# Seven block products for eight in two of the four out-projection chunks of batches 2 to 7

## The chip, the cores and the metric

One Trainium2 chip, one of its cores. The kernel is one launch on that core. The metric is the device time of a run in microseconds; the profile is one further execution of the same program, with its own time.

## The reference

Eight batches of attention with a pack of 32 learned queries per head, and then a feed-forward layer with the activation h cos h:

```
scale = 1/sqrt(64)
sm_attn(q, k, v) = softmax(scale * q k^T) v
p_packed = sm_attn(p, k, v)             # p: 8 x 8 x 32 x 64;  k, v: 8 x 8 x 576 x 64
attn     = sm_attn(q, p_packed, p_packed)
x        = attn as 4608 x 512           # tokens x (heads * 64)
h        = x @ w_in                     # w_in 512 x 2048
out      = (h * cos(h)) @ w_out         # w_out 2048 x 512, output float32
```

## The kernel before, in words

Work goes batch by batch (576 tokens, eight heads). Everything is emitted in an order written out by hand: each engine takes its instructions in the order of the program, and tile pools add the waits. Matmul operands are bf16, sums fp32.

Per batch s:

- `load` (L84) brings k, q and v from HBM through GpSimd's DMA queue; `permute_v` (L77) reorders v on GpSimd into `vp`; `xbar` (L93) and `a1_xbar` (L156) transpose q, k and the first attention weights by DMA from SP's queue.
- `s1` (L129, L140): scores of the packed queries and their exponentials on ScalarE. `recips` (L151, L152): the inverse row sums r1 on VectorE, and rs1 = r1 * scale, also on VectorE. `pp` (L183): the packed values, copied to `ppT`.
- `ppw` (L207): packed values times w_in, in four blocks n of 512 columns, evacuated to `PPW` by L75 (ScalarE) or L77 (VectorE). So x @ w_in is never formed; the hidden product uses PPW.
- `s2` (L129, L225): scores of the queries, exponentials `a2u`. `sums2` (L233, L235): their sums per head by a matmul with a block of ones, and the logarithm in `lns` (SBUF, fp32). `normalise` (L241, L243): exp(-lns) on ScalarE, then a2n = a2u * r1 * that on VectorE, for the halves y = 0 and 1.
- `h_mm` (L256, L260, L263), 16 times, fc = 0 to 15: four matmuls of 288 columns to a `psA` tile, cos by ScalarE (a sine with a bias) and the product g = h cos h by VectorE to `gT` [128, 16, 576]. After fc 7 and 15 GpSimd copies the last 64 tokens to `joint` (L267), which holds the remainders of two batches.
- The out-projection, `out_gen` (L309): chunks of 128 tokens, each 16 matmuls of 512 columns over the 2048 hidden features, into an `ot` bank; then a copy to `osb` by ScalarE or VectorE and stores on SP's queue (L316). Odd batches have a fifth chunk, the joint one. The last joint chunk is done at the end in two column halves (`tail_chunk`, L295).

PSUM holds three `psA` tiles of two banks (pool A) and two `ot` banks (pool O). The out-projection of batch s-1 fills in between the steps of batch s: `fill(n)` emits its next n matmuls. Slot s is the loop at L523 and the function `slot` (L423): in the first part come s2, the last PPW blocks, s1 of batch s+1, sums2 and normalise, with fills between them; then 16 hidden products with fills after each, in proportion to a quota, and with hooks: at fc 5 `pp(s+1)`, at fc 10 two PPW blocks of batch s+1. `keep` fills are left for the start of the next slot, where `set_filler` finishes them and begins the next batch's.

```
        normalise(s)
        ACT.preload_act_table_set(SIN_SET)
        fill(13)
...
        slot(s, [(5, lambda: pp(s + 1, engs=(ACT, ACT))), (10, lambda: pw2(s + 1))] if nxt else [], 5, {10: 3})
```

Before batch 3 the slots are written out one by one, with more loads and transposes.

Of the kernel before, what the change touches and what calls it, by code (L numbers as in the profile page):

```python
# [15 lines left out]
def kernel(  # L16
# [10 lines left out]
    nc = tc.nc  # L27
    B, H, S, D = q.shape
# [5 lines left out]
    TP = S // C  # L34
    HS = S // 2
    PSUM = bass.MemoryType.PSUM
    EXP_SET = "natural_log_exp_and_others"
    SIN_SET = "trig_and_small"

    const = ctx.enter_context(tc.tile_pool(name="const", bufs=1))  # L40
    bf_pool = ctx.enter_context(tc.tile_pool(name="bf", bufs=1))
    vp_pool = ctx.enter_context(tc.tile_pool(name="vp", bufs=2))
    att_pool = ctx.enter_context(tc.tile_pool(name="att", bufs=1))
    a2n_pool = ctx.enter_context(tc.tile_pool(name="a2n", bufs=2))
    ppw_pool = ctx.enter_context(tc.tile_pool(name="ppw", bufs=2))
    g_pool = ctx.enter_context(tc.tile_pool(name="g", bufs=2))
    j_pool = ctx.enter_context(tc.tile_pool(name="joint", bufs=2))
    cos_pool = ctx.enter_context(tc.tile_pool(name="cos", bufs=3))
    o_pool = ctx.enter_context(tc.tile_pool(name="o", bufs=4))
# [8 lines left out]
    w_out_bf = const.tile([128, NFC, DM], BF16, name="w_out_bf")  # L58
    ident = const.tile([128, 128], BF16, name="ident")
# [3 lines left out]
    p_raw = const.tile([128, 2 * B, D], FP32, name="p_raw")  # L63
# [84 lines left out]
    def recips(b):  # L148
        r1[b] = small.tile([128, 2], FP32, name="r1")
        rs1[b] = small.tile([128, 2], FP32, name="rs1")  # L150
        V.reciprocal(r1[b], sums1[b])  # L151
        V.tensor_scalar(out=rs1[b], in0=r1[b], scalar1=scale, scalar2=None, op0=ALU.mult)  # L152
# [42 lines left out]
    def ppw(b, n, eng=None, own=False, later=False, cuts=((0, 512),)):  # L195
        if b not in PPW:
            PPW[b] = ppw_pool.tile([128, 2, DF], BF16, name="PPW", tag="PPW")
# [12 lines left out]
        def evacuate(cuts=cuts):  # L210
            if own or two:
                for a, z in cuts:
                    for y in range(2):
                        copy(eng[y] if two else eng, PPW[b][:, y, n * 512 + a:n * 512 + z], ps[y][:, a:z])
            else:
                copy(eng or (V, ACT)[n % 2], PPW[b][:, :, n * 512:(n + 1) * 512], t)
# [4 lines left out]
    def s2(b):  # L221
        a2u[b] = att_pool.tile([128, 2, S], BF16, name="a2u", tag="a2u")
        ps = scores(ppT[b % 2], xT["q", b])
        for y in range(2):
            ACT.activation(out=a2u[b][:, y].rearrange("p (e x) -> p e x", e=2),  # L225
                           in_=ps[y][:, :, 0:HS], func=AF.Exp, scale=rs1[b][:, y:y + 1])

    def sums2(b, y):
        if b not in lns:
            lns[b] = att_pool.tile([128, 2, S], FP32, name="lns", tag="lns")  # L230
        ps = psa()
        for e in range(2):
            nc.tensor.matmul(ps[:, e, 0:HS], ones_blk, a2u[b][:, y, e * HS:(e + 1) * HS],  # L233
                             start=True, stop=True)
        ACT.activation(out=lns[b][:, y].rearrange("p (e x) -> p e x", e=2),  # L235
                       in_=ps[:, :, 0:HS], func=AF.Ln)

    def normalise(b):
        a2n[b] = a2n_pool.tile([128, 2, S], BF16, name="a2n", tag="a2n")
        for y in range(2):  # L240
            ACT.activation(out=lns[b][:, y], in_=lns[b][:, y], func=AF.Exp, scale=-1.0)  # L241
        for y in range(2):
            V.scalar_tensor_tensor(out=a2n[b][:, y], in0=a2u[b][:, y], scalar=r1[b][:, y:y + 1],  # L243
                                   in1=lns[b][:, y], op0=ALU.mult, op1=ALU.mult)
# [3 lines left out]
    def h_mm(b, fc):  # L248
        if fc == 0:
            gT[b] = g_pool.tile([128, NFC, S], BF16, name="gT", tag="gT")  # L250
# [3 lines left out]
        for y in range(2):  # L254
            for e in range(2):
                nc.tensor.matmul(ps[:, e, 0:HS], PPW[b][:, y, fc * 128:(fc + 1) * 128],  # L256
                                 a2n[b][:, y, e * HS:(e + 1) * HS], start=(y == 0), stop=(y == 1))
        cs = cos_pool.tile([128, S], BF16, name="cosT")
# [12 lines left out]
    n_out, out_eng = [0], [V, ACT]  # L271

    def pieces_of(b, c):
        ob = out[b * S:(b + 1) * S, :].rearrange("(p c) d -> c p d", c=C)
        if c == 4:
            o0 = out[(b - 1) * S:b * S, :].rearrange("(p c) d -> c p d", c=C)
# [9 lines left out]
    def n_chunks(b):  # L286
        return 5 if b % 2 and b < B - 1 else 4

    def tail_chunk(b, c):
        osb = o_pool.tile([128, DM], FP32, name="osb")  # L290
        for i in range(2):
            cols = slice(i * 256, i * 256 + 256)
            ps = O.tile([128, 256], FP32, name="ot", tag="ot")
            for fc in range(NFC):
                nc.tensor.matmul(ps, joint[b // 2][:, fc, :], w_out_bf[:, fc, cols],  # L295
                                 start=(fc == 0), stop=(fc == NFC - 1))
            copy((ACT, V)[i], osb[:, cols], ps)
            for (a, z, rows), q in zip(pieces_of(b, c), (nc.sync, nc.scalar)):
                q.dma_start(out=rows[:, cols], in_=osb[a:z, cols])

    def out_gen(b):
        groups = [(0, 1), (2,), (3,)] if b == 0 else [(c,) for c in range(n_chunks(b))]
        for grp in groups:
            pss = {c: O.tile([128, DM], FP32, name="ot", tag="ot") for c in grp}
            for f0 in range(0, NFC, 4):
                for c in grp:
                    for fc in range(f0, f0 + 4):
                        w = joint[b // 2][:, fc, :] if c == 4 else gT[b][:, fc, c * 128:(c + 1) * 128]
                        nc.tensor.matmul(pss[c], w, w_out_bf[:, fc, :],  # L309
                                         start=(fc == 0), stop=(fc == NFC - 1))  # L310
                        if fc == NFC - 1:
                            osb = o_pool.tile([128, DM], FP32, name="osb")
                            copy(out_eng[n_out[0] % len(out_eng)], osb, pss[c])
                            n_out[0] += 1
                            for a, z, rows in pieces_of(b, c):
                                nc.sync.dma_start(out=rows, in_=osb[a:z, :])  # L316
                        yield
# [3 lines left out]
    def set_filler(b):  # L321
        fill(1000)
        filler[0] = out_gen(b)
        filler[1] = 16 * n_chunks(b)

    def fill(n):
        while n > 0 and filler[1] > 0:
            next(filler[0])
            filler[1] -= 1
            n -= 1  # L330

# [243 lines left out]
```

The softmax here doesn't subtract the row's maximum and nothing guards it: scores larger than these inputs give would overflow.

## Time and profile before

| | |
|---|---|
| time, median of 2 runs | 248.99 us (248.95 to 249.03) |
| profiled execution, its own time | 248.62 us |
| its span, first to last instruction | 246.8 us |
| granted TensorE clock | 1.00 |
| busy: TensorE, VectorE, ScalarE, GpSimd | 233.2, 165.2, 169.0, 57.7 us |
| out-projection matmul, 128x512 | 379 ns each, first input to last output |
| hidden matmul, 128x288 | 286 ns each |
| g = h cos h on VectorE, 128x576 | 755 ns each |
| cos on ScalarE, 128x576 | 652 ns each |
| osb copy 128x512: VectorE, ScalarE | 690, 581 ns |
| osb copy 128x256: VectorE, ScalarE | 424, 372 ns |
| PPW cast 128x1024 on VectorE | 1222 ns |
| permute_v on GpSimd, 96x3072 | 2751 ns |
| joint copy on GpSimd, 128x512 | 616 ns |

PE is TensorE's matmuls, PEld its weight loads, DVE is VectorE, ACT ScalarE, POOL GpSimd, SP the engine that issues most DMAs. Matmuls overlap, so the time of one is longer than the distance between two. A row of the timeline gives start, duration, engine, line, operation, the tiles written and read, and how many of them in sequence; in brackets, the idle time before it and who ended it.

### The profile page before, as it was taken

What the parts mean: (1) busy time and instruction counts of PE and PEld (TensorE: products, weight loads), DVE (VectorE), ACT (ScalarE), POOL (GpSimd) and SP (SyncE); (2) the same over time, 40 slices, a digit from 0 to 9 for tenths busy, and PEclk for the clock granted to TensorE, in tenths of its full rate; (3) what the DMA queues carried; (4) which work ended last, traced back from release to release, by engine and by line L of the source; (5) the groups of instructions that cost most, each with busy time, mean ns of one, the idle gap of its engine ahead of it and who ended that gap; (6) DMA issues with size and microseconds to landing.
All of it is one profiled execution on the core that took longest, in us unless ns stands there. A gap on an engine that the chain in (4) does not pass through costs nothing.

```text
span 246.8 us, 5023 instructions
## 1 busy us (share of the span) xinstructions
PE 233.2 (94%) x1996; PEld 130.9 (53%) x2029; DVE 165.2 (67%) x248; ACT 169.0 (68%) x282; POOL 57.7 (23%) x70
## 2 busy tenths in 40 slices
PE   8788799999999999999999999999999999999993
PEld 3454374566545654565446554565456554665452
DVE  3549987677658776678767766678766684886110
ACT  2369799877576787888787776888778684873000
POOL 8342533240400355004503105030500100001000
PEclk9999999999999999999999999999999999999999
DMA  6999999999899999999999997999571113111133
GB/s 90 202 203 206 205 206 228 194 241 151 179 202 184 192 175 214 218 198 142 222 211 187 172 201 91 198 166 171 109 154 27 45 43 84 43 31 57 47 84 85
DMA packets 64231, 37.36 MB, mean 151 GB/s; under 512 B 36848, under 2 KB 59632, under 8 KB 64208
## 3 DMA queue, kind: packets, MB, share of 16 engines
q0 software_dynamic: 23152, 18.75, 50.0%
q1 hardware_dynamic: 40624, 18.09, 35.1%
q8 instruction: 16, 0.26, 0.4%
q10 hardware_dynamic: 432, 0.20, 0.4%
q14 instruction: 7, 0.06, 0.1%
HBM read 37.22 MB, written 9.44 MB: 189 GB/s over the span
## 4 chain that ended last, share of the span: by engine, by line
PE 78%; DMA 12%; issue 2%; DVE 2%; ACT 2%; POOL 2%; DVEq 0%; POOLq 0%
PE ot L309 46%; PE psA L256 21%; DMA vbf<-in_v_dram 10%; PE psA L207 3%; DMA a1T<-a 2%; PE psA L129 2%; PE psA L183 2%; DVE gT L263 2%; PE ot L295 1%; PE psA L233 1%; ACT cosT L260 1%; POOL vp L77 1%; ACT ppT L75 1%; POOL kbf L84 1%; PE ot L104 0%
## 5 line engine op out<-in xcount | busy, mean ns | idle before, releaser
L309 PE MATMUL ot<-w_out_bf,gT 128*128 128x512 bf16 x482 | 127.5, 379 | 2.0 <-issue 1.1
L263 DVE TENSOR_TENSOR gT<-psA,cosT 128x576 bf16<-128x576 f32 x128 | 93.8, 755 | 28.9 <-ACT cosT L260 28.2
L260 ACT ACTIVATE cosT<-psA 128x576 bf16<-128x576 f32 x128 | 82.4, 652 | 24.6 <-PE psA L256 22.1
L256 PE MATMUL psA<-a2n,PPW 128*128 128x288 bf16 x512 | 83.8, 286 | 1.6 <-DVE gT L263 0.4
L309 PEld LDWEIGHTS <-gT 128*128 128x128 bf16 x512 | 47.8, 98 | 43.4 <-issue 6.7
L256 PEld LDWEIGHTS <-PPW 128*128 128x128 bf16 x512 | 49.3, 98 | 34.6 <-issue 3.9
L77 DVE CAST PPW<-psA 128x1024 bf16<-128x1024 f32 (+1 forms) x23 | 26.9, 1175 | 11.6 <-PE psA L207 11.5
L267 POOL COPY joint<-gT 128x512 bf16<-128x512 bf16 x16 | 9.9, 616 | 82.5 <-DVE gT L263 82.5
L77 DVE COPY osb<-ot 128x512 f32<-128x512 f32 (+1 forms) x22 | 14.9, 678 | 17.5 <-PE ot L309 7.7
L77 POOL COPY vp<-vbf 96x3072 bf16<-96x3072 bf16 x7 | 19.3, 2751 | 6.3 <-DMA vbf<-in_v_dram 6.3
L75 ACT COPY osb<-ot 128x512 f32<-128x512 f32 (+1 forms) x15 | 8.5, 567 | 15.3 <-PE ot L309 10.6
L243 DVE SCALAR_TENSOR_TENSOR a2n<-a2u,r,lns 128x576 bf16<-128x576 bf16 x16 | 12.3, 812 | 7.3 <-ACT lns L241 7.3
L235 ACT ACTIVATE lns<-psA 128x576 f32<-128x576 f32 x16 | 10.1, 650 | 7.1 <-PE psA L233 6.5
L140 ACT ACTIVATE a<-psA 128x576 bf16<-128x576 f32 x16 | 10.3, 647 | 6.7 <-PE psA L129 6.7
L309 PE MATMUL ot<-w_out_bf,joint 128*128 128x512 bf16 x47 | 12.8, 379 | 0.1
L225 ACT ACTIVATE a2u<-psA,rs 128x576 bf16<-128x576 f32 x16 | 11.0, 737 | 1.4 <-PE psA L129 1.3
L75 ACT CAST ppT<-psA 64x128 bf16<-64x128 f32 x24 | 6.2, 260 | 7.0 <-DVE ppT L77 5.9
L207 PE MATMUL psA<-w_in_bf,ppT 64*32 64x512 bf16 x224 | 10.1, 380 | 0.0
L241 ACT ACTIVATE lns<-lns 128x576 f32<-128x576 f32 x16 | 10.0, 676 | 0.0
L347 PE MATMUL ot<-wz 128*128 128x512 bf16 x23 | 7.7, 468 | 1.4 <-DVE wz L358 1.2
L527 POOL COPY gate<-kT 1x1 bf16<-1x1 bf16 x3 | 0.5, 181 | 32.3 <-DMA kT<-kbf 32.3
L183 PEld LDWEIGHTS <-vp 96*128 96x128 bf16 x192 | 6.5, 98 | 2.3 <-issue 1.2
(73 smaller groups left out, 152.7 us busy)
## 6 DMA issues: line engine op xcount, KB each, us to landing
kbf<-in_k_dram POOLq DMA_DIRECT2D x8, 576.0 KB, 12.6
vbf<-in_v_dram POOLq DMA_DIRECT2D x8, 576.0 KB, 7.6
qbf<-in_q_dram POOLq DMA_DIRECT2D x8, 576.0 KB, 10.1
out_dram<-osb SPq DMA_DIRECT2D x24, 192.0 KB, 2.7
out_dram<-osb SPq DMA_DIRECT2D x22, 128.0 KB, 2.4
w_in_bf<-in_moe_w_in_dram POOLq DMA_DIRECT2D x4, 512.0 KB, 17.3
w_out_bf<-in_moe_w_out_dram POOLq DMA_DIRECT2D x4, 512.0 KB, 21.2
out_dram<-osb SPq DMA_DIRECT2D x26, 64.0 KB, 2.1
```

The costliest lines, as they stand in the source:

```text
L75: ACT.copy(out=out, in_=in_)
L77: eng.tensor_copy(out=out, in_=in_)
L140: ACT.activation(out=a1[b % 2][:, y, :, 0:TP].rearrange("p (e m) x -> p e m x", e=2), in_=ps[y][:, :, 0:HS].rearrange("p e (m x) -> p e m ...
L183: nc.tensor.matmul(ps[:, hp * 64:(hp + 1) * 64], vp[b][:, c, hp * 128:(hp + 1) * 128], a1T[b][0:TP, :, j, 32 * hp:32 * hp + 32], start=(j ...
L207: nc.tensor.matmul(ps[y][32 * x:32 * x + 32, :], ppT[b % 2][r, 2 * x + y, :], w_in_bf[r, x, n * 512:(n + 1) * 512], start=True, stop=True)
L225: ACT.activation(out=a2u[b][:, y].rearrange("p (e x) -> p e x", e=2), in_=ps[y][:, :, 0:HS], func=AF.Exp, scale=rs1[b][:, y:y + 1])
L235: ACT.activation(out=lns[b][:, y].rearrange("p (e x) -> p e x", e=2), in_=ps[:, :, 0:HS], func=AF.Ln)
L243: V.scalar_tensor_tensor(out=a2n[b][:, y], in0=a2u[b][:, y], scalar=r1[b][:, y:y + 1], in1=lns[b][:, y], op0=ALU.mult, op1=ALU.mult)
L256: nc.tensor.matmul(ps[:, e, 0:HS], PPW[b][:, y, fc * 128:(fc + 1) * 128], a2n[b][:, y, e * HS:(e + 1) * HS], start=(y == 0), stop=(y == 1))
L260: ACT.activation(out=csv, in_=ps[:, :, 0:HS], func=AF.Sin, bias=PI_HALF)
L263: V.tensor_tensor(out=gT[b][:, fc, :].rearrange("p (e x) -> p e x", e=2), in0=ps[:, :, 0:HS], in1=csv, op=ALU.mult)
L309: nc.tensor.matmul(pss[c], w, w_out_bf[:, fc, :], start=(fc == 0), stop=(fc == NFC - 1))
```

## The change

**Block products.** For batches 2 to 7 (`FIRST = 2`), chunks 0 and 1 (256 tokens) are computed together. With the hidden features split in even and odd fc and the output columns in two halves of 256, the product is one of 2x2 blocks, and seven block products with sums before and after take the place of eight. A block product is 8 matmuls of 256 columns. Chunks 2 and 3 stay as they were; batches 0 and 1 stay as they were.

- Sums of w_out's blocks (T0 to T3, 2048 elements per partition each) are made once, on GpSimd, in slots 1 and 2; T3 takes over the buffer of `p_raw`.
- Sums of g's blocks (S1 to S4) are made per batch on GpSimd by `S_sums`, in two parts of 512 elements per partition each, so eight instructions, in `close`, right before the next batch's fills are set and before `permute_v`. For the last batch, parts of them come at fc 7 and 11 of slot 7.
- `pair_gen` emits the products in the order 1, (2, 6), 7, (4, 5), 3, each group in one `ot` bank. Product 1 is copied to `m1`; the others are combined by VectorE sums that read PSUM and an SBUF operand (`plus`).

**Order of the out-projection.** A batch's fills are now: one column half of a joint chunk (batches 1 to 6), the direct chunks, then the pair. `fill` counts half passes: 2 for a 512-column matmul, 1 for a 256-column one. `keep` is 10 halves (5 passes before). In a slot the fills are emitted before the product g where there is no hook.

**Other edits.** rs1 = r1 * scale is made by ScalarE (`scaled`), at hook 2 of the slot before. From batch 3 on the logarithms and inverse sums stay in PSUM, in place of `lns`. The two halves of a2n are emitted after 4 and 8 of 13 fills, not together. PPW is four tiles of 512 columns rather than two of 2048; `vp` has one buffer rather than two. From batch 2 on the copy of a chunk is on VectorE in the first part of a slot and on ScalarE in the hidden products, as before, and at the end on ScalarE alone.

The core of the diff:

```diff
-    vp_pool = ctx.enter_context(tc.tile_pool(name="vp", bufs=2))
+    vp_pool = ctx.enter_context(tc.tile_pool(name="vp", bufs=1))
-    ppw_pool = ctx.enter_context(tc.tile_pool(name="ppw", bufs=2))
+    ppw_pool = ctx.enter_context(tc.tile_pool(name="ppw", bufs=4))
...
+    def scaled(b):
         rs1[b] = small.tile([128, 2], FP32, name="rs1")
-        V.reciprocal(r1[b], sums1[b])
-        V.tensor_scalar(out=rs1[b], in0=r1[b], scalar1=scale, scalar2=None, op0=ALU.mult)
+        ACT.activation(out=rs1[b], in_=r1[b], func=AF.Copy, scale=scale)
...
+        else:
+            lns[b, y] = ps[:, :, 0:HS]
...
+    def S_sums(b, p, eng, k0, k1, which=(0, 1, 2, 3)):
...
+        t = S[b, p]
+        A11, A12 = (A_blk(b, 2 * p, i, k0, k1) for i in range(2))
+        A21, A22 = (A_blk(b, 2 * p + 1, i, k0, k1) for i in range(2))
+        S1, S2, S3, S4 = (t[:, i, k0:k1, :] for i in range(4))
+        for i in which:
+            out, in0, in1, op = ((S1, A21, A22, ALU.add), (S2, S1, A11, ALU.subtract),
+                                 (S3, A11, A21, ALU.subtract), (S4, A12, S2, ALU.subtract))[i]
+            eng.tensor_tensor(out=out, in0=in0, in1=in1, op=op)
...
+    def pair_gen(b, p):
...
+        m = {1: (A11, B_blk(0, 0)), 2: (A12, B_blk(1, 0)), 3: (S4, B_blk(1, 1)),
+             4: (A_blk(b, 2 * p + 1, 1, 0, 8), T[3]), 5: (S1, T[0]), 6: (S2, T[1]), 7: (S3, T[2])}
+
+        def then_double(ps):
+            plus(o2, ps, u3)
+            store(o2, 2 * p + 1)
+            plus(o1[:, 2], ps[:, 1], o1[:, 2])
+
+        def then_last(ps):
+            plus(o1[:, 1], ps, o1[:, 2])
+            store(o1, 2 * p)
+
+        then = {1: lambda ps: copy(out_eng[0], m1, ps), 2: lambda ps: plus(o1[:, 0:3:2, :], ps, m1),
+                7: lambda ps: plus(u3, ps, o1[:, 2]), 4: then_double, 3: then_last}
+
+        for names in ((1,), (2, 6), (7,), (4, 5), (3,)):
+            ps = O.tile([128, 2, 256], FP32, name="ot", tag="ot")
+            for i, n in enumerate(names):
+                lhs, rhs = m[n]
+                for kp in range(8):
+                    nc.tensor.matmul(ps[:, i], lhs[:, kp, :], rhs[:, kp, :], start=kp == 0, stop=kp == 7)
+                    if kp == 7 and n == names[-1]:
+                        then[names[0]](ps if i else ps[:, 0])
+                    yield 1
...
+    def out_gen(b):
+        for j, i in joints_of(b):
+            yield from joint_half(j, i, store_half(j))
+        if b < FIRST:
+            yield from direct_gen(b, ((0, 1), (2,), (3,)) if b == 0 else ((0,), (1,), (2,), (3,)))
+        else:
+            yield from direct_gen(b, ((2,), (3,)))
+            yield from pair_gen(b, 0)
...
-            h_mm(s, fc)()
+            rest = h_mm(s, fc)
...
+            if not (hooks and hooks[0][0] == fc):
+                fill_halves(quota)
+                rest()
...
+    def close(s):
+        fill(1000)
+        if s >= FIRST:
+            for g in ((6, 8),) if s == B - 1 else ((0, 4), (4, 8)):
+                S_sums(s, 0, G, *g)
+        set_filler(s)
...
-        fill(1000)
-        set_filler(s - 1)
+        close(s - 1)
         if nxt:
             permute_v(s + 1)
...
-        normalise(s)
+        product = normalise(s, later=True)
         ACT.preload_act_table_set(SIN_SET)
-        fill(13)
+        fill(4)
+        product(0)
+        fill(4)
+        product(1)
+        fill(5)
...
-        slot(s, [(5, lambda: pp(s + 1, engs=(ACT, ACT))), (10, lambda: pw2(s + 1))] if nxt else [], 5, {10: 3})
+        slot(s, [(2, lambda: scaled(s + 1)), (5, lambda: pp(s + 1, engs=(ACT, ACT))), (10, lambda: pw2(s + 1))] if nxt else [], 10, {10: 3})
```

`plus(out, in0, one)` is a VectorE tensor_tensor add of a PSUM tile and an SBUF tile, the latter broadcast over two column halves where needed.

## The prediction, made before the changed kernel ran

> **What bounds the kernel now.** I read the totals first, then the chain of work that ended last, then busy time by window, then the timeline where batches meet. Totals and chain of the kernel before:
>
> ```profile
> PE 233.2 (94%) x1996; PEld 130.9 (53%) x2029; DVE 165.2 (67%) x248; ACT 169.0 (68%) x282; POOL 57.7 (23%) x70
> ...
> PE ot L309 46%; PE psA L256 21%; DMA vbf<-in_v_dram 10%; PE psA L207 3%; DMA a1T<-a 2%; PE psA L129 2%; PE psA L183 2%; DVE gT L263 2%; PE ot L295 1%; PE psA L233 1%; ACT cosT L260 1%; POOL vp L77 1%; ACT ppT L75 1%; POOL kbf L84 1%; PE ot L104 0%
> ```
>
> TensorE carries the chain, and nearly half of it is the out-projection (L309). By window (window, length, then busy time of each engine), slots 4 and 5:
>
> ```profile
> 120.30:148.60 28.30, 27.87 (x233) 15.46 (x228) 19.40 (x26) 21.18 (x36) 6.49 (x8) 1.00 1.08 190
> 148.60:173.80 25.20, 24.91 (x217) 14.07 (x220) 18.92 (x26) 20.27 (x35) 5.50 (x6) 1.00 0.87 153
> ```
>
> TensorE idles 0.3 to 0.4 us in 25 to 28; VectorE has about 6 us to spare. So a microsecond taken from TensorE is worth a microsecond, if VectorE, in the new order, releases its buffers on time. Pass lengths, from the timeline of the end, where nothing else runs on TensorE:
>
> ```profile
> 225.78 13.33 PE L309 MATMUL ot<-w_out_bf,gT 128*128 128x512 bf16 x60
> 239.16 3.66 PE L295 MATMUL ot<-w_out_bf,joint 128*128 128x256 bf16 x32
> ```
>
> A 512-column pass has a latency of 0.379, so its pitch is (13.33-0.38)/59 = 0.219; a 256-column pass: (3.66-0.272)/31 = 0.109. Half the columns cost half.
>
> Two seams matter. First, the second denominator of batch 5 up to its first hidden product:
>
> ```profile
> 154.23 0.41 PE L233 MATMUL psA<-a2u,ones_blk 128*128 128x288 bf16 x2
> ...
> 155.22 1.25 ACT L241 ACTIVATE lns<-lns 128x576 f32<-128x576 f32 x2
> 155.93 1.55 DVE L243 SCALAR_TENSOR_TENSOR a2n<-a2u,r,lns 128x576 bf16<-128x576 bf16 x2 [1.46 <-ACT lns L241]
> ...
> 157.28 0.53 PE L256 MATMUL psA<-a2n,PPW 128*128 128x288 bf16 x3
> 157.48 0.69 DVE L77 COPY osb<-ot 128x512 f32<-128x512 f32 x1
> ```
>
> The normalisation ends at 157.48; the third matmul of the hidden product, which reads its second half, is due at 157.28 + 2 x 0.12 = 157.53. There is no slack left. Second, the close of slot 4:
>
> ```profile
> 146.29 0.65 PE L256 MATMUL psA<-a2n,PPW 128*128 128x288 bf16 x4
> 147.66 0.76 DVE L263 TENSOR_TENSOR gT<-psA,cosT 128x576 bf16<-128x576 f32 x1 [0.16 <-ACT cosT L260]
> 148.48 0.61 POOL L267 COPY joint<-gT 128x512 bf16<-128x512 bf16 x1 [9.36 <-DVE gT L263]
> 148.60 0.44 PE L129 MATMUL psA<-qT,ppT 64*32 64x288 bf16 x16
> 149.03 2.75 POOL L77 COPY vp<-vbf 96x3072 bf16<-96x3072 bf16 x1
> 161.80 0.86 PE L183 MATMUL psA<-a1T,vp 96*128 96x64 bf16 x24
> ```
>
> The last product g of a slot is written 2.13 us after its hidden product starts (146.29 to 148.42). vp is ready at 151.8, 10 us before TensorE reads it.
>
> [...]
>
> **The change, part by part.**
>
> *Products.* In each of six batches 32 passes of 512 (32 x 0.219 = 7.00) become 56 of 256 (56 x 0.109 = 6.12). Saved 0.88, times 6: **-5.3**. The joint chunks go from 48 passes of 512 to 96 of 256: 10.5 either way. Batches 0 and 1 are as before. Weight loads take 98 ns and kept pace with 109 at the end, so they cost nothing.
>
> *VectorE, amount.* Per pair two osb copies (0.69, on either engine) become one 0.42 copy on ScalarE in the slot and five sums, two of 512 and three of 256 columns. One PSUM input runs at the pace of the copies (0.69 and 0.42): 2.6 us. The score scale leaves VectorE (-0.17 to -0.23) for ScalarE (about +0.2). About +2 us of 6 to spare: no cost by amount. The cost comes from order, in five places.
>
> (a) *Normalisation split.* In the built order of VectorE, chunk 2's osb copy now stands between the two halves of a2n. The chunk is finished 10 half passes after the second denominator, 0.25 + 1.09 + 0.16 = 1.5 after its start, before the first half ends at 1.7 + 0.75. So the second half is 0.69 late, less some 0.1 for reading PSUM (755 for 812 ns) and hand-overs. TensorE stands before the third matmul: 0.55 x 5 (batches 3 to 7) + 0.8 (batch 2): **+3.5**. Cover: none, by the first seam. ScalarE's first sine is late with it.
>
> (b) *Banks at the seam.* Two ot banks alternate, so the next batch's joint half takes the bank of products 4 and 5. Their two sums (0.69 + 0.42) queue behind the last g: 2.13 + 1.11 = 3.25 after the last hidden product's start. TensorE is there at 0.49 + 14 half passes (1.53) + scores and one PPW block (0.75): 2.8. **+1.8** (0.45 in slots 4 to 7). Behind the sums wait two PPW casts, not urgent.
>
> (c) *Products 4 and 5 themselves* need the bank of 2 and 6, whose sum stands behind the 1.22 PPW cast of hook 10: g at 2.13, cast 3.32, sum 4.0 from the slot's tenth hidden product; TensorE arrives at about 3.8. **+0.8** (0.2 x 4).
>
> (d) *End.* At the close of slot 7 no scores intervene: chunk 2 of batch 7 waits until 3.25 where TensorE is there at 2.05: 1.2. In the tail the joint half needs products 4 and 5 cleared (0.16 + 0.69 + 0.42 + hand-overs) while product 3 takes 0.87: 0.4. **+1.6**.
>
> (e) *GpSimd.* Eight sums of 512 elements go ahead of permute_v, and four T sums of 2048 into slots 1 and 2. The trace has no such operation. Lower bound: the copy of 512, 0.62. [...] I take 1.25. From the scores: joint copy done at about 0.8, sums 10 plus 0.35 of waits between dependent ones, permute 2.75: vp at 13.9 + 0.1. TensorE wants it at 8.7 (first part) + 6 hidden products 2.94 + 16 half passes 1.75 = 13.4, plus (a) and (b) = 14.4. Hidden from slot 4 on. In slot 3 the T3 sum [...] delays the joint copies and (b) is absent: **+0.7** (0 to 2). The loads queued behind permute_v and the kT gate (161.61 before) shift by under 1 us and land 3 us before use. T0 and T1 end at about 64.3 after the 52.5 permute, before the gate opened anyway (64.91). One vp buffer: its reader was a slot earlier. SP carries two more stores ahead of a1T's transpose, some 1.2 us; a1T still lands about 3 us before its product. At the lower bound of 0.62 only the +0.7 goes.
>
> TensorE's idle time of 0.3 a slot is partly the same waits (a psA wait after the packed product): **-0.5**. PPW in four 512 tiles and the fill-before-product order add no pass; no cost.
>
> Sum: -5.3 +3.5 +1.8 +0.8 +1.6 +0.7 -0.5 = **+2.6**. The profiled execution: span 246.8 + 2.6 = 249.4, with 1.8 around it (248.62 - 246.8) 251.2; the median of the runs shown is 0.4 above that execution: 248.99 + 2.6 = **251.6**.
>
> **Rivals.**
> *The waits are shorter than I place them.* For: VectorE has 6 us to spare per slot, and each wait is a difference of 0.2 to 0.6 between two sums. [...] If only half of (a) to (d) is real (3.9), the change is -5.3 + 3.9 + 0.2 - 0.5 = -1.7; with none it is 243.7. Around 246.5.
> *GpSimd becomes the bound (the slower side).* Place: the packed product of hook 5 in slots 3 to 6, waiting for vp. Each 0.1 us on a sum costs 0.8 a slot, four slots. It starts to cost at 1.31; at 1.38 the total passes 254.0, 2% above; at 1.5: 8 x 0.19 x 3 + 8 x 0.25 - 0.7 = +5.9: 257.5. For: nothing in the trace bounds it from above, and vp's 10 us of slack is just what the sums use up. [...]
> *Narrow passes don't run at half price* between hidden products. At 0.122, the pace of the 288-column ones, the saving shrinks from 5.3 to 1.0: 255.9. Against: the 109 ns row.
>
> **How the numbers follow.** Forecast 0.50, with its own range 249 to 254; short waits 0.28 (243.5 to 249); GpSimd bound 0.17 (254 to 262); narrow passes 0.05. 2% is about what a measurement of this kernel tells from no change, so the limits are 244.0 and 254.0. Faster: the bottom of the second case, 0.03. Slower: most of the third and fourth and a little of the first, 0.20. Same: 0.77. The 8-in-10 range leaves out some 0.07 below and 0.10 above: 245.5 to 257.
>
> **What would show it.** Products: the new 256-column rows at a pitch of 0.109. (a): idle time on TensorE before the hidden products, released by VectorE's normalisation, some 0.5 a batch. (b) to (d): idle time before the joint half and the new products, released by VectorE's sums. (e): one GpSimd sum at 1.2 to 1.3; much above 1.3, and a wait of TensorE for vp, the second rival is true. TensorE busy throughout, with a span below 245, would make the prediction wrong.

## The result, and the profile after

The changed kernel takes 258.01 us (median of two runs, 257.38 and 258.64) where the kernel before takes 248.99: a ratio of 1.036 (1.025 to 1.047). It is slower, by more than the forecast of 251.6 and by 1.0 us more than the range reached. The profiled execution took 258.64 us with a span of 256.9, so the comparison by parts below has 256.9 - 246.8 = 10.1 us to explain.

Totals and chain of the changed kernel (line numbers are its own: L354 is the direct out-projection, L406 the block products, L332 the joint half, L272 the hidden product, L379 the sums of block products):

```profile
PE 233.5 (91%) x2199; PEld 151.0 (59%) x2221; DVE 171.2 (67%) x264; ACT 169.2 (66%) x293; POOL 128.4 (50%) x126
...
PE psA L272 15%; PE ot L354 12%; PE ot L406 10%; DMA p_raw<-in_p_dram 8%; DMA w_in_bf<-in_moe_w_in_dram 7%; PE ot L332 6%; ACT cosT L276 3%; POOL T L299 3%; DVE gT L279 3%; DVE osb L379 2%; DVE a2n L255 2%; PE psA L212 2%; ACT ppT L79 2%; DVE osb L81 2%; ACT osb L79 1%
```

TensorE's busy time did not fall (233.2 before), though it has 5.3 us less to do; part of it ran at a lower clock (0.66 and 0.50, below), and busy times of matmuls overlap (0.379 us from first input to last output of a 512-column pass, at a pitch of 0.219), so this total says little here. The chain is no longer TensorE's alone; VectorE's sums (L379), a2n (L255) and GpSimd's T sums (L299) stand in it. Slots 4 and 5, each from its s2 to the next (window, length, busy time of PE, PEld, DVE, ACT and POOL):

```profile
127.72:154.98 27.26, 26.12 (x260) 18.01 (x262) 20.34 (x31) 20.77 (x37) 15.39 (x15) 1.00 0.94 167
154.98:182.18 27.20, 26.11 (x259) 18.02 (x261) 20.34 (x31) 20.76 (x37) 14.63 (x14) 1.00 0.81 146
```

Before, the two were 28.42 and 25.22 (s2 of slot 4 starts at 120.18, so the prediction's first window begins 0.12 late), on average 26.8 with a joint chunk in every second one. Now each has half a joint chunk and takes 27.2: 0.4 more, where products alone should have brought 0.9 less. TensorE idles 1.1 us in each. The list of TensorE's waits (engine, tile and line, released by what: us in total, times, longest) names the places:

```profile
PE ot L332 <- POOL joint L283: 3.8, 2, 2.9
PE psA L272 <- DVE a2n L255: 2.7, 6, 0.5
PE ot L332 <- DVE osb L379: 1.6, 5, 0.3
...
PE ot L354 <- DVE osb L379: 0.9, 1, 0.9
```

The second, third and fourth were forecast (of the five waits of the third, four are the seams of slots 4 to 7 and one, 0.24, is in the tail). The first was not. It lies at the start of slot 2, in the timeline of GpSimd and TensorE:

```profile
60.84 4.07 POOL L299 TENSOR_TENSOR T<-w_out_bf,T 128x2048 bf16<-128x2048 bf16 x1
...
64.85 0.61 POOL L283 COPY joint<-gT 128x512 bf16<-128x512 bf16 x1
65.52 1.05 PE L332 MATMUL ot<-w_out_bf,joint 128*128 128x256 bf16 x8 [0.85 <-POOL joint L283]
65.95 0.18 POOL L568 COPY gate<-kT 1x1 bf16<-1x1 bf16 x1 [0.49 <-DMA kT<-kbf]
...
68.79 0.62 POOL L283 COPY joint<-gT 128x512 bf16<-128x512 bf16 x1
69.47 0.39 PE L332 MATMUL ot<-w_out_bf,joint 128*128 128x256 bf16 x2 [2.91 <-POOL joint L283]
```

The joint half now opens batch 1's output. It needs GpSimd's two joint copies of slot 1. The first (64.85) stands behind the T sums; the second (68.79) behind the gate on kT and three loads, which the program has at fc 12, before it. TensorE waits 0.85 and 2.91 us. What follows its restart is seen in the windows (the granted clock is third from the right):

```profile
70.00:72.00 2.00, 2.00 (x17) 1.54 (x16) 1.34 (x4) 0.00 (x0) 2.00 (x1) 0.66 1.31 202
72.00:74.00 2.00, 1.78 (x27) 1.48 (x26) 0.16 (x1) 0.00 (x0) 1.43 (x1) 0.50 1.34 212
```

The clock was 1.00 up to 70 us and 0.99 from 74 on: soon after the wait TensorE runs at half speed. From its restart at 69.47 to s2 of batch 2 at 75.60 it took 6.13 us; in the fourth experiment below, which waits as long and kept its clock, the same work took 4.50 us (68.25 to 72.75). So the waits cost 3.8 us and the clock after them 1.6. The kernel before has the same order on GpSimd:

```profile
64.91 0.18 POOL L443 COPY gate<-kT 1x1 bf16<-1x1 bf16 x1 [9.14 <-DMA kT<-kbf]
...
67.73 0.62 POOL L267 COPY joint<-gT 128x512 bf16<-128x512 bf16 x1
```

Its joint copy came as late after slot 2's first scores (4.7 us, 4.6 in the changed kernel), but there the joint chunk came last in batch 1's output, and no wait followed.

### The profile page after: what moved, and what is told of

It is laid out like the page before. It is cut to its first block, busy times and chain, and to the rows that moved or that the text cites. A ratio compares the mean times of both kernels' runs of the same rounds, so it can differ in the third digit from the quotient of the medians.

```text
span 256.9 us, 5545 instructions
## 1 busy us (share of the span) xinstructions
PE 233.5 (91%) x2199; PEld 151.0 (59%) x2221; DVE 171.2 (67%) x264; ACT 169.2 (66%) x293; POOL 128.4 (50%) x126
## 4 chain that ended last, share of the span: by engine, by line
PE 48%; DMA 17%; DVE 9%; ACT 8%; POOL 8%; issue 7%; SPq 0%; DVEq 0%; ACTq 0%; POOLq 0%
PE psA L272 15%; PE ot L354 12%; PE ot L406 10%; DMA p_raw<-in_p_dram 8%; DMA w_in_bf<-in_moe_w_in_dram 7%; PE ot L332 6%; ACT cosT L276 3%; POOL T L299 3%; DVE gT L279 3%; DVE osb L379 2%; DVE a2n L255 2%; PE psA L212 2%; ACT ppT L79 2%; DVE osb L81 2%; ACT osb L79 1%
## 5 line engine op out<-in xcount | busy, mean ns | idle before, releaser
L272 PE MATMUL psA<-a2n,PPW 128*128 128x288 bf16 x512 | 84.4, 286 | 4.7 <-DVE a2n L255 2.7
L354 PE MATMUL ot<-w_out_bf,gT 128*128 128x512 bf16 x300 | 80.4, 381 | 2.4 <-DVE osb L379 0.9
L272 PEld LDWEIGHTS <-PPW 128*128 128x128 bf16 x512 | 49.1, 97 | 29.1 <-issue 8.6
L354 PEld LDWEIGHTS <-gT 128*128 128x128 bf16 x320 | 30.2, 98 | 28.2 <-issue 4.6
L81 DVE CAST PPW<-psA 128x1024 bf16<-128x1024 f32 (+1 forms) x23 | 26.8, 1174 | 7.6 <-PE psA L212 7.3
L313 POOL TENSOR_TENSOR S<-gT 128x512 bf16<-128x512 bf16 (+1 forms) x26 | 28.1, 1081 | 7.4 <-PE ot L406 7.4
L332 PE MATMUL ot<-w_out_bf,joint 128*128 128x256 bf16 x128 | 15.9, 275 | 5.4 <-POOL joint L283 3.8
L406 PEld LDWEIGHTS <-S 128*128 128x128 bf16 x192 | 18.5, 98 | 3.8 <-issue 1.3
L406 PE MATMUL ot<-T,S 128*128 128x256 bf16 x144 | 20.0, 273 | 0.0
L332 PEld LDWEIGHTS <-joint 128*128 128x128 bf16 x128 | 12.2, 98 | 8.9 <-POOL joint L283 4.3
L255 DVE SCALAR_TENSOR_TENSOR a2n<-a2u,r,psA 128x576 bf16<-128x576 bf16 x10 | 8.1, 810 | 12.4 <-ACT psA L251 12.4
L406 PEld LDWEIGHTS <-gT 128*128 128x128 bf16 x144 | 13.8, 98 | 3.0
L406 PE MATMUL ot<-w_out_bf,gT 128*128 128x256 bf16 x96 | 14.7, 273 | 0.0
L313 POOL TENSOR_TENSOR S<-S,gT 128x512 bf16<-128x512 bf16 (+1 forms) x13 | 14.0, 1079 | 1.0
L313 POOL TENSOR_TENSOR S<-gT,S 128x512 bf16<-128x512 bf16 (+1 forms) x13 | 14.0, 1078 | 0.0
```

The costliest lines, as they stand in the source:

```text
L81: eng.tensor_copy(out=out, in_=in_)
L255: V.scalar_tensor_tensor(out=v[0], in0=v[1], scalar=r1[b][:, y:y + 1], in1=lns[b, y], op0=ALU.mult, op1=ALU.mult)
L272: nc.tensor.matmul(ps[:, e, 0:HS], PPW[b, fc // 4][:, y, fc % 4 * 128:fc % 4 * 128 + 128], a2n[b][:, y, e * HS:(e + 1) * HS], start=(y == ...
L313: eng.tensor_tensor(out=out, in0=in0, in1=in1, op=op)
L354: nc.tensor.matmul(pss[c], gT[b][:, fc, c * 128:(c + 1) * 128], w_out_bf[:, fc, :], start=(fc == 0), stop=(fc == NFC - 1))
L406: nc.tensor.matmul(ps[:, i], lhs[:, kp, :], rhs[:, kp, :], start=kp == 0, stop=kp == 7)
```

## The experiments

My theory from this profile: 5.4 us come from slot 2's joint half, the rest from the seams that the prediction named. The rivals: GpSimd's sums slow the kernel as a whole, or block products don't pay on TensorE. In each expectation A is the theory and B its rival; the letter beside a result says which of them its number fits. Each experiment was timed beside the kernel before on the same chip, which took 248.28 to 248.95 us there.

| kernel | us, median (lowest to highest) | ratio to before |
|---|---|---|
| changed kernel | 258.01 (257.38 to 258.64) | 1.036 (1.025 to 1.047) |
| 1 joint half last in batch 1 | 253.27 (252.55 to 253.61) | 1.018 (1.016 to 1.021) |
| 2 halves of a2n together | 254.54 (252.09 to 255.54) | 1.022 (1.017 to 1.028) |
| 3 no S sums | 257.74 (257.47 to 258.51) | 1.037 (1.035 to 1.040) |
| 4 no block products | 258.49 (256.12 to 259.50) | 1.038 (1.033 to 1.044) |
| 5 = 1 and 2 | 250.68 (249.58 to 251.77) | 1.007 (1.004 to 1.010) |
| 6 = 5, and the seam moved | 252.90 (252.65 to 253.06) | 1.016 (1.014 to 1.018) |
| 7 = 5, no block products | 250.85 (250.19 to 251.26) | 1.008 (1.006 to 1.010) |
| 8 late loads | 252.68 (252.48 to 253.01) | 1.016 (1.014 to 1.017) |
| 9 joint half last in all, and 2 | 248.70 (248.10 to 249.53) | 1.001 (1.000 to 1.002) |
| 10 joint half last in all | 249.16 (248.88 to 249.46) | 1.003 (1.002 to 1.005) |
| 11 = 9, no block products | 249.70 (249.22 to 250.98) | 1.005 (1.003 to 1.008) |
| 12 = 9, casts of pp shared | 251.91 (251.60 to 252.17) | 1.013 (1.011 to 1.015) |
| 13 = 9, two sums out | 247.09 (246.71 to 248.03) | 0.993 (0.991 to 0.996) |
| 14 = 9, PPW casts on ScalarE | 248.91 (248.72 to 249.46) | 1.003 (1.002 to 1.004) |
| 15 = 9, g ahead of its fills | 248.33 (247.77 to 249.15) | 1.000 (0.999 to 1.001) |
| 16 = 14 and 15 | 248.81 (248.36 to 249.65) | 1.002 (1.001 to 1.003) |

**1. Joint half last in batch 1.**

```diff
         for j, i in joints_of(b):
-            yield from joint_half(j, i, store_half(j))
+            if b > 1:
+                yield from joint_half(j, i, store_half(j))
         if b < FIRST:
             yield from direct_gen(...)
+            if b == 1:
+                yield from joint_half(1, 0, store_half(1))
```

> Only edit: in the fills of slot 2 the joint half of batches 0 and 1 comes after the four direct chunks of batch 1, not before them. Theory A (TensorE waited 0.85 + 2.91 us for the joint copy, which stands on GpSimd behind the block sums, the kT gate and three loads; the granted clock then fell to 0.50 to 0.66 for some 4 us, another 1.7): the wait and the low clock both go, 258.0 becomes about 252.4. Rival B (the clock fell, or the time went, for another cause; the joint half's wait only shows it): the wait moves to the next instruction, 256 to 258.

253.27: 4.7 us less. In the profiled execution s2 of batch 2 starts at 69.30 (75.60 in the changed kernel, 68.87 before), with no wait for the joint copies and the clock at 1.00 throughout. Theory A, 0.9 us short of its number.

**2. Both halves of a2n together** (slots 2 to 7; the same in slot 2's own code).

```diff
-        fill(4)
-        product(0)
-        fill(4)
-        product(1)
-        fill(5)
+        product(0)
+        product(1)
+        fill(13)
```

> Only edit: both halves of the normalised weights are emitted together, before the fills, in slots 2 to 7, so that no osb copy stands between them on VectorE. Theory A (each slot's third hidden matmul waits 0.5 us for the second half behind the osb copy): 0.45 x 6 = 2.7 less, 255.3. Rival B (the wait moves to the osb copy's bank, or ScalarE was the limit anyway): 257.5 to 258.5.

254.54: 3.5 less, A. The wait for a2n is gone from the list. The profiled execution still has the joint wait in slot 2 and a longer fall of the clock after it (to 0.50 for some 5 us), and its runs follow the clock: 252.09 at a mean clock of 1.00, 253.89 at 0.99, 255.20 and 255.54 at 0.983. So the 3.5 is uncertain. Two cleaner figures: experiment 5 below is experiment 1 with this edit, and takes 2.6 us less (250.68 for 253.27); and from s2 of batch 2 on, where both profiled executions have the full clock, each stretch from one s2 to the next is 0.60 us shorter than in the changed kernel, the last one 0.55: 3.6 in all.

**3. No S sums.** In `S_sums` nothing is emitted, and the products read g's own blocks.

> Leaves out the GpSimd sums of g's blocks (S1 to S4): the products read plain blocks of g instead, as many passes of the same shape; the output is not the reference's. Theory A (the sums at 1.16 us each are hidden behind the fills; vp is ready 1.9 us before it is read): within 0.7 of 258.0. Rival B (GpSimd is the bound: vp late, or its sums slow VectorE): 254 or less.

257.74, within 0.3 us of the changed kernel. GpSimd's busy time falls from 128.4 to 73.7 us and the kernel's time does not follow; that rival falls.

**4. No block products.** `FIRST = 8`; T and S sums are left out with them.

> No block products: all batches use the direct chunks, and no sums are made on GpSimd; every other edit of the change stays (joint halves first, score scale on ScalarE, inverse sums in PSUM, split normalisation, one vp buffer). Theory A: the products' saving of 5.3 is lost, the bank waits at the seams and at the end (0.35 x 4 + 1.2 = 2.6) and the 0.85 from the T sums go, the 2.9 wait in slot 2 with some 1 to 2 us of low clock and the normalisation waits stay: 258.0 + 5.3 - 2.6 - 0.9 = 259.8. Rival B (the block products are the costly part): 252 or less.

258.49: A's number is 1.3 us too high, but B is refuted: without block products no run came near 252. Its runs differ by the clock, too: 256.12 in the profiled execution, which kept it (0.999), 258.40 to 259.50 in the others (0.983 to 0.993). It also shows what slot 2 waits for, since here GpSimd has no T sums at all:

```profile
64.74 0.18 POOL L568 COPY gate<-kT 1x1 bf16<-1x1 bf16 x1 [8.84 <-DMA kT<-kbf]
...
67.57 0.62 POOL L283 COPY joint<-gT 128x512 bf16<-128x512 bf16 x1
...
68.25 0.39 PE L332 MATMUL ot<-w_out_bf,joint 128*128 128x256 bf16 x2 [3.37 <-POOL joint L283]
```

GpSimd is idle for 8.84 us, and the joint copy is as late: it stands behind a gate that waits for a DMA, and three loads.

**5. Edits 1 and 2 together.**

> Two edits of the changed kernel together: in batch 1's output the joint half last instead of first, and both halves of the normalised product issued together before the fills (slots 2 to 7). A, the two costs are separate (slot 2's wait for GpSimd's joint copies, 4.7 us as measured alone; the wait for a2n in six slots, 2.7 us by the trace): 250.0 to 250.9, with neither wait in the list of waits and s2 of batch 2 starting near 69.3. B, they hide each other or the time comes back as another wait later in the slot: 252 or more.

250.68, A: neither cost hides the other, and together they make 7.3 us of the changed kernel's loss.

**8. Late loads.** The joint half first, as in the changed kernel; only GpSimd's order is changed.

```diff
-             (12, next_loads)], 8, {3: 3})
+             ], 8, {3: 3})
+    next_loads()
     T_sums(2, G)
```

> The changed kernel with one move: the gate on kT and the three loads of slot 1 issued after the slot's last joint copy on GpSimd in place of before it; joint half first, T sums where they were. A, slot 2's long wait comes from the joint copy standing behind the gate and the loads in GpSimd's order (2.9 us of the 3.8, and the clock's fall after it): 253.3 to 255, one wait for joint of 0.9 to 1.5 us left. B, it comes from the two T sums of 4.06 us ahead: 257.5 to 258.5.

252.68, A, and even below its range. Timeline of slot 2's start:

```profile
59.70 4.06 POOL L299 TENSOR_TENSOR T<-w_out_bf,T 128x2048 bf16<-128x2048 bf16 x1
63.70 1.17 POOL L283 COPY joint<-gT 128x512 bf16<-128x512 bf16 x2
64.37 1.26 PE L332 MATMUL ot<-w_out_bf,joint 128*128 128x256 bf16 x10
65.32 0.18 POOL L568 COPY gate<-kT 1x1 bf16<-1x1 bf16 x1 [0.45 <-DMA kT<-kbf]
```

Both joint copies follow each other, the long wait is gone though the T sums stand where they stood, and the gate opens no later than in the changed kernel (65.95; the kernel before had 64.91). The place of four GpSimd instructions was worth 5.3 us.

**6. The seam: 8 held back for 10, and ppw later.**

```diff
         s2(s)
-        ppw(s, 2, V)
         if nxt:
             xbar("q", s + 1)
-        fill(10)
+        fill(8)
+        ppw(s, 2, V)
+        fill(2)
```

> As the kernel with both edits (joint half last in batch 1, both a2n halves together), and two more: 8 held back for the seam in place of 10, so that products 4 and 5 end before the last g and their sums stand ahead of it on VectorE, and the first ppw of the seam after eight of the joint half's matmuls in place of before them. A, the seam's wait is only the place of the last g ahead of the two sums (0.35 us in five slots, 0.9 us before chunk 2 of batch 7): 2.6 us less than with the two edits, 247.6 to 248.4. B, the last g then comes 1.1 us late and its PSUM buffer holds up the seam's ppw or the scores: no gain, or up to 1 us slower than with the two edits.

252.90: B, and worse than B put it. The waits at the banks went (0.2 us left before the joint half, 0.3 before chunk 2), but the second ppw of the seam then waits 0.44 us in four slots for the first one's cast, TensorE waits 1.1 us in all for late g products, and the last joint copy comes 0.3 us late in two. A stall moved.

**7. Edits 1 and 2, no block products.**

> As the kernel with both edits, with the block products, T and S sums left out (all four chunks of every batch directly); the output is the reference's. A, with the two costs gone the block products bring their 5.3 us less what the banks at the seam take (1.6 + 0.9 + 0.2 us) and a few tenths of small waits: this kernel 2.0 to 3.0 us slower than with the two edits, about 253. B, they bring nothing (as the earlier kernel without them, 258.49 against 258.01, would have it): within 0.7 us of the kernel with the two edits.

250.85 against 250.68: B. My working, 5.3 less the seam's 2.7, missed something worth some 2.4 us.

**9, 10 and 11. The joint half last in every batch.** The fills held back for the seam then are the joint half's, and chunk 2 opens the seam on a bank long free.

```diff
     def out_gen(b):
-        for j, i in joints_of(b):
-            yield from joint_half(j, i, store_half(j))
         if b < FIRST:
...
             yield from pair_gen(b, 0)
+        for j, i in joints_of(b):
+            yield from joint_half(j, i, store_half(j))
```

> The changed kernel with both halves of a2n issued together, and the joint half last in every batch's output, not in batch 1's alone: the ten matmuls held back for the seam are then the joint half's, products 4, 5 and 3 end 1.75 us earlier inside the slot, and chunk 2 of the next batch opens the seam on a bank that has long been free. A, the seam's wait is a matter of which chunk stands there: the wait of 0.35 us in five slots and of 0.9 us before chunk 2 of batch 7 goes, 2.7 us off the 250.7 of the kernel with both edits, 247.6 to 248.8. B, the sums of products 4, 5 and 3 now stand among the g products on VectorE and hold up psA there, as the seam edit with 8 held back did: 250 or more.

> As the kernel with the joint half last in every batch, but the two halves of a2n split by fills as in the changed kernel. A, the wait for a2n comes from chunk 2's copy standing between the halves on VectorE: chunk 2 now ends 1.75 us earlier, before either half, so no copy splits them, and the time is within 0.5 us of the kernel with both halves together. B, it comes from the split itself, the second half issued late: 2.5 us slower than that kernel.

> As the kernel with the joint half last in every batch and both halves of a2n together, with the block products, T and S sums left out (all four chunks directly); the output is the reference's. A, with the seam's waits gone the block products bring what they save on TensorE, 5.3 us less a few tenths a slot of waits for psA: 2.5 to 4.5 us slower than with the products, about 251. B, they bring nothing for another reason than the seam (ScalarE or VectorE set the pace of the slot): within 0.8 us.

9 takes 248.70, A's number and within 0.2% of the kernel before. But not for A's reason alone: its slots 4 to 6 take 26.71, 26.64 and 26.64 us, those of kernel 5, which still wait 0.35 us at each seam, 26.65, 26.59 and 26.59. In the slots the seam's wait came back in another place (B); the profiled executions show the gain in the last stretch, from s2 of batch 7 to the end (46.9 us to 45.7), and 0.2 in slot 3. 10 takes 249.16: A; only slot 2 still waits for a2n (0.3 us), so in the changed kernel the wait came from chunk 2's copy between the halves. 11 takes 249.70: neither. Without any of the waits found so far, block products bring 1.0 us of 5.3. Where that is: from s2 of batch 3 to s2 of batch 7, kernel 9 takes 106.75 us and kernel 11 106.98, so four batches bring 0.06 us each; from s2 of batch 7 to the end, 45.70 and 46.52, so the last stretch, in which no next batch is prepared, brings 0.8. Two windows in slot 5's second half, for kernel 9 and then for kernel 11:

```profile
164.99:167.99 3.00, 2.82 (x34) 1.59 (x31) 3.00 (x6) 1.68 (x3) 0.61 (x1) 1.00 1.31 203
170.99:174.49 3.50, 3.46 (x32) 2.57 (x30) 3.50 (x6) 2.71 (x4) 0.00 (x0) 1.00 0.47 114
```

```profile
165.56:168.56 3.00, 3.00 (x32) 1.50 (x30) 2.56 (x4) 2.28 (x4) 0.61 (x1) 1.00 1.30 200
171.56:175.06 3.50, 3.50 (x29) 2.56 (x27) 2.90 (x5) 3.15 (x6) 0.00 (x0) 1.00 0.10 26
```

With block products VectorE (the third busy time) is full, 3.00 of 3.00 and 3.50 of 3.50, and TensorE is not; without them it is the other way round. Where TensorE is held in kernel 9:

```profile
165.33 0.49 PE L406 MATMUL ot<-T,S 128*128 128x256 bf16 x3
...
166.01 0.66 PE L272 MATMUL psA<-a2n,PPW 128*128 128x288 bf16 x4 [0.18 <-DVE gT L279]
```

Three passes of 0.109 from 165.33 would let the hidden product start at 165.66; it starts 0.35 late. (The list shows less, 0.18, because it counts idle time from the end of the last matmul, 165.82, and a matmul's 0.272 is longer than the pitch.) Counted in this way there are three such delays in slot 5, 0.35, 0.19 (in the PPW blocks from 167.26) and 0.20 (at 171.54), 0.74 of the 0.88 us saved. Each waits for a psA buffer that a product g frees, and each of these g stands on VectorE behind a sum of block products.

Kernel 11 also shows what the rest of the change costs: it has the change's other edits (but for the split of a2n and the joint half's place), none of the products and none of the waits named so far, and takes 1.3 us more than the kernel before beside it (249.70 for 248.37). Which edit costs that was not tested.

**13. Two of VectorE's five sums out.**

```diff
-            plus(o2, ps, u3)
+            plus(o2, ps, m1)
             store(o2, 2 * p + 1)
-            plus(o1[:, 2], ps[:, 1], o1[:, 2])
...
-                7: lambda ps: plus(u3, ps, o1[:, 2]), 4: then_double, 3: then_last}
+                7: lambda ps: None, 4: then_double, 3: then_last}
```

> As the kernel with the joint half last in every batch and both halves of a2n together, with two of the five sums of a pair of chunks left out on VectorE (u3, and the one from the second bank of products 4 and 5: 0.42 us each; chunk 1 then takes m1 in its place, so the output is not the reference's). TensorE's work is the same. A, VectorE's load is where the products' 0.88 us a slot stays: 0.4 to 0.8 us less in each of six slots, 244 to 246.5. B, TensorE sets the pace: within 0.6 us of 248.7.

247.09, 1.6 us less than kernel 9: the direction of A, short of its range. Slots 4 to 6 take 26.31, 26.24 and 26.24 us for 26.71, 26.64 and 26.64: 0.40 each for 0.84 us less on VectorE, with the same work on TensorE. Of the three delays of slot 5 the last two, 0.39 in all, are gone; they stood behind the two sums left out. Slot 3 gave 0.5 back, with a wait of 0.8 us of pp for a psA buffer.

**12 and 14. The casts shared otherwise.** 12 has `pp(s + 1)`, with two casts by VectorE, for `pp(s + 1, engs=(ACT, ACT))`; 14 has `pw2(s + 1, 0, ACT)` for `pw2(s + 1)`.

> As the kernel with the joint half last in every batch and both halves of a2n together, with one move: in slots 2 to 6 the four casts of pp's PSUM to ppT are shared, two by VectorE and two by ScalarE, in place of four by ScalarE, since the trace shows VectorE idle for 1.07 us while ScalarE makes them and the next cosine waits. The output is the reference's. A, the chain of ScalarE's cosine and VectorE's product sets the pace of a slot's second half (VectorE busy 3.00 of 3.00 us there): 0.2 to 0.4 us less in each of five slots, 246.7 to 247.7. B, TensorE sets it after all: within 0.4 us of 248.7.

> As the kernel with the joint half last in every batch and both halves of a2n together, with one move: in slots 2 to 6 both PPW casts of the slot's hook are made by ScalarE, in place of one by VectorE (1.21 us) and one by ScalarE (1.01 us), so that VectorE has 1.2 us less in the stretch in which it is full. The output is the reference's. A, VectorE's load alone sets the pace of the second half: as with two sums left out (0.84 us off VectorE gave 0.40 us a slot), 0.4 to 0.6 us less in each of five slots, 245.7 to 246.9. B, ScalarE's cosines stand behind the second cast and are late by as much: 248.5 or more.

12 takes 251.91: both theories miss. In kernel 9 the casts took ScalarE from 162.15 to 163.22 and the next cosine began at 163.25, 2.00 us after pp. In kernel 12 (pp at 163.31) they did not run side by side:

```profile
160.03 4.88 DVE L279 TENSOR_TENSOR gT<-psA,cosT 128x576 bf16<-128x576 f32 x6 [0.55 <-ACT cosT L276]
...
164.83 0.58 DVE L81 CAST ppT<-psA 64x128 bf16<-64x128 f32 x2
165.50 0.53 ACT L79 CAST ppT<-psA 64x128 bf16<-64x128 f32 x2 [1.38 <-DVE ppT L81]
166.06 1.73 ACT L276 ACTIVATE cosT<-psA 128x576 bf16<-128x576 f32 x3
```

VectorE comes to its casts after six g products, ScalarE to its own after VectorE's, and the cosine 2.75 us after pp: 0.75 later, and slots 3 to 6 are each 0.74 to 0.75 longer. 14 takes 248.91, B's number, but not for B's reason. The cast that left VectorE had stood between its two full stretches, not in them: in slot 5, 165.47 to 168.47 and 171.47 to 174.97, VectorE is as full as in kernel 9, and between them it now idles until products 4 and 5 end:

```profile
170.29 0.69 DVE L379 TENSOR_TENSOR osb<-ot,u 128x512 f32<-128x512 f32 x1 [1.52 <-PE ot L406]
```

**15 and 16. Each g ahead of its fills**, as in the kernel before, alone and with edit 14.

```diff
-                fill_halves(quota)
                 rest()
+                fill_halves(quota)
```

> As the kernel with the joint half last in every batch and both halves of a2n together, with one edit of the change undone: in a slot each product g is issued before the fills that follow its hidden product, not after them, so that a sum of block products that ends in those fills stands behind that g on VectorE. The output is the reference's. A, the place of the sums ahead of a g, not VectorE's load, is what holds up psA: 0.3 to 0.6 us less in each of five slots, 245.7 to 247.2. B, the load sets the pace whatever the order, or the sums now come late for their banks: within 0.5 us of 248.7, or slower.

> As the kernel with each g issued before its fills, and both PPW casts of the slot's hook by ScalarE as well. A, with the order mended VectorE's load is what is left, and 1.2 us less of it a slot gives 0.2 to 0.5 us a slot more than the order alone. B, no load left to ease: within 0.5 us of the kernel with the order alone.

15 takes 248.33: B. Slots 5 and 6 take 26.49 for 26.64, so the place of the sums ahead of a g is worth 0.15 us a slot, not 0.3. 16 is 0.5 us slower than 15: B. Kernel 15 is the best version that does the whole work, and equal to the kernel before (0.999 to 1.001); no version that does the whole work beats it.

## Why the prediction was wrong

By its own terms, in the profiled executions:

| term | forecast | measured |
|---|---|---|
| products on TensorE | -5.3 | -5.3 (pitch of 256 columns 0.109) |
| (a) normalisation split | +3.5 | +3.6 (slots against experiment 2; the list of waits has 2.7) |
| (b) bank at the seam | +1.8 | +1.4 (four waits of 0.35) |
| (c) products 4 and 5 | +0.8 | no wait listed |
| (d) end | +1.6 | +1.2 (0.94 and 0.24) |
| (e) GpSimd, slot 3 | +0.7 | no wait of TensorE for vp (ready at 113.6, read at 114.95) |
| slot 2's joint half, and the clock | 0 | +5.4 |
| up to slot 2's first scores (62.99 before, 64.23 after) | 0 | +1.2 (63.39 to 64.01 in the experiments; cause open) |
| rest, with the -0.5 | -0.5 | +2.6 |
| sum | +2.6 | +10.1 |

**The step that failed** is one sentence of (e): "T0 and T1 end at about 64.3 after the 52.5 permute, before the gate opened anyway (64.91)." It asked what the T sums do to the loads, and found the loads covered. The 64.3 rested on my own estimate of a T sum, with no such operation in the trace of before; the time was nearly right (two sums of 4.06 and 4.07 us, T1 ended at 64.91). But the joint copies stand in the same queue, and the change had moved their reader from the end of batch 1's output to its front. The prediction priced the joint half's place at the later seams (its bank), and at slot 2 not at all. Experiments 1 and 8 show 4.7 and 5.3 us for it. The cause of the long wait is not even the T sums (only the 0.85 before it stands behind them), but the order gate, loads, joint copy, which the kernel before had already and which cost nothing as long as the joint chunk came last.

**The second failure** is "About +2 us of 6 to spare: no cost by amount." That was an average over the slot. The sums fall into its second half, where they and the g products fill VectorE (experiments 9 and 11). There 0.8 of the 0.88 us that TensorE saves in a slot is given back, as waits for psA behind late g products; two sums fewer return 0.40 of it (13), their order 0.15 (15). How the remainder divides between VectorE's load and the hand-over from cosine to g is not settled: taking casts away helped neither (12, 14, 16). In the changed kernel itself I cannot separate this from (a) and (b), whose waits give VectorE time. It may be part of the rest of 2.6 us, as may the other edits (1.3 in kernel 11) and the parts of (b) and (d) that the list doesn't count; what is shown of it is shown in the kernels without those waits.

**Right:** (a) in mechanism and in size. Slot 5's normalisation in the changed kernel:

```profile
162.74 0.81 DVE L255 SCALAR_TENSOR_TENSOR a2n<-a2u,r,psA 128x576 bf16<-128x576 bf16 x1 [2.47 <-ACT psA L251]
...
163.47 0.68 DVE L81 COPY osb<-ot 128x512 f32<-128x512 f32 x1
...
164.07 0.81 DVE L255 SCALAR_TENSOR_TENSOR a2n<-a2u,r,psA 128x576 bf16<-128x576 bf16 x1
...
164.93 0.41 PE L272 MATMUL psA<-a2n,PPW 128*128 128x288 bf16 x2 [0.44 <-DVE a2n L255]
```

The copy stands between the halves, and TensorE waits 0.44 after its last matmul's end, which delays it by the 0.60 that experiment 2 gives back, for 0.55 forecast. (b) is there as forecast, 0.35 for 0.45, behind the sums that stand behind the last g (to remove it, in kernel 9, gave nothing back in slots 4 to 6):

```profile
182.12 0.68 DVE L379 TENSOR_TENSOR osb<-ot,u 128x512 f32<-128x512 f32 x1
...
182.71 0.94 DVE L379 TENSOR_TENSOR osb<-ot,osb 128x256 f32<-128x256 f32 x2
183.18 1.91 PE L332 MATMUL ot<-w_out_bf,joint 128*128 128x256 bf16 x16 [0.35 <-DVE osb L379]
```

GpSimd's sum takes 1.156 us for 512 elements; the 1.25 of (e) was my own estimate, which no trace of before showed. The longest took 1.162, so none was drawn out by what VectorE did beside it. So vp is ready at 167.5 and read at 169.41 in slot 5. The rivals: GpSimd as the bound is false, and so are narrow passes at a higher price. "The waits are shorter" is true in part: (a) to (d) come to 6.2 us for 7.7, with (a) as long as forecast, and that was outweighed by what wasn't in the sum. Two slips in the prediction's sums change nothing of this: without (a) to (d) its own terms give 243.4, not 243.7; and they pass 254.0 at a sum of 1.39 us, not 1.38.

## What to carry to other kernels

When a change moves a reader to the front of a queue of work, follow each of its inputs back through its own engine's program order, gates and DMA issues too, not only through the resource that the change adds load to. Room on an engine is to be counted in the stretch where the new work falls, and along the chain in which it stands, not over the stage. Before moving an instruction out of a full stretch, look whether it really lies in that stretch, and who stands behind it on the engine that takes it over: experiments 6, 12 and 14 only moved the stall, and so did experiment 9 at the seams of slots 4 to 6.

## What the hardware showed that I had not expected

In the changed kernel TensorE's waits of 3.8 us cost nearly half as much again through its clock (1.6 us, by the comparison with experiment 4). After 2.91 us without a matmul, with 0.85 us of waiting shortly before, the granted clock fell to 0.50 and pp took 1.49 us for 0.86. It does not follow from the wait's length alone: the profiled execution of experiment 4 waited 3.37 us and kept 1.00, those of experiments 3 and 2 waited 3.3 and 3.28 us, with TensorE busy for 4.00 of 4.00 us from 60 to 64, and fell to 0.50, in experiment 2 for about 5 us after the wait. Reading the inverse sums from PSUM made VectorE's a2n no faster: 810 ns, as with both operands in SBUF (812 ns).
